# Inputs and output laid out by numpy, a row per partition for each transfer, in a memory attention and mixer kernel

## The chip, the cores and the metric

The kernel runs on 1 core of one Trainium2 chip. The metric is the device time of one execution in microseconds (us); the host's work before and after it, numpy's included, is not in it.

## The reference, cut to what matters

```
a    = softmax(phi, over the sequence)              # phi (8, 8, 576, 32)
k_m  = einsum('bhsm,bhsd->bhmd', a, k)              # q, k, v (8, 8, 576, 64)
v_m  = einsum('bhsm,bhsd->bhmd', a, v)
attn = softmax(q @ k_m.T / 8, over the 32 memories)
x    = (attn @ v_m) as (8, 576, 512)                # heads side by side
h    = relu(x.T @ w_tok1) @ w_tok2                  # 576 -> 256 -> 576
u    = x + h.T
out  = u + relu(u @ w_ch1) @ w_ch2                  # 512 -> 1536 -> 512
```

There are 8 batches of 8 heads. The inputs q and k are scaled up by 64 and phi by 3.18; the four weights arrive as float64.

## The kernel before

**Numbers.** Each large matmul is made of three, with a high and a low part of each operand (`uh`/`ul`, `c1h`/`c1l`, `hh`/`hl` and so on). ACT rounds the high part, DVE or POOL subtracts it for the low part. A float64 weight is read as pairs of 32-bit words, and five passes over 1024 pairs put one fp32 number together (class `Piece`): `low_bits` (ACT, L667), `join` (DVE, L673), `signs` (ACT, L679), `magnitude` (DVE L685 or ACT L683) and `apply` (DVE, L690). Then `part_high` (ACT, L697) and `part_low` (POOL or DVE, L701) split it.

**Heads.** The four heads of one batch with the same parity Q are a `Quad`. It goes through: maximum of phi over the sequence (`_red`, L310; turned on PE and reduced, `phi_turn` L983, `phi_diag` L987 and L989, `phi_spread` L993), subtraction (`phi_sub`, L324), exp; the memories `kvp` from k, v and phi (`mm_kv`, L1002); their scaling, `T` and `vb` (L369 to L409); the keys, turned on PE (`Tp`, L1012) and copied to `kb` (L1016); the scores `sp` from q and `kb` (L1047); softmax on DVE (`S`, L466 to L496); and the token mixer (`nat`, `A`, `R`, `u`), which writes u as `uh` and `ul` (L624, L630).

**Rows.** The 4608 rows of u go through the channel mixer in 9 chunks of 512 (`Chunk`). `ch1` makes one of 12 products `cp` in 12 matmuls of 128x512 (L157), ACT and DVE take its relu as `hh` and `hl`, and `ch2` adds it into four sums `acc` (12 matmuls, L190). At a chunk's end `add` (L208) makes the output `o`, channels on partitions. `turn` (L214) transposes it into `rows` on DVE, and `store` (L224) sends it with 4 DMAs.

**The order.** Every load is issued by SP, in one queue. In the first part (batches 0 and 1, the weights, chunk 0) each operation is a `step` with an engine, a cost in us, steps that it comes after, buffers that it takes (`Room`), and for a load a `move`, the time that its bytes are thought to need. `plan(SEED)` sorts them: it runs a clock over the engines, takes the ready step of highest rank, and adds a random share to the ranks, drawn from `SEED`. `SHARES` says how often a step goes to its other engine. Where the plan has a gap on PE, matmuls of `ident` with itself fill it (L949). What comes after chunk 0 follows a table by hand, `at(h, fn)`, at half-steps h of the products; `run` works it off.

**Transfers.** q of the first two batches lands with the sequence on partitions; `q_turn` transposes it on PE (L1024 into `qp`, the last 64 rows at L1029 into `qt`), and `q_get` copies it to `qT` on ACT (L1036, L1037). Later batches load q in 16 DMAs of 36 KB, and DVE transposes it. The 576 rows of k, v and phi are 4.5 times 128, and so each is loaded as a body and a tail, k apart from v. w_ch1 comes in four DMAs of 32 partitions a piece. The last chunk is done in two halves: four times matmuls, `add` and `turn`, then four DMAs, two from SP's queue and two from ACT's.

Of the kernel before, what the change touches and what calls it, by code (L numbers as in the profile page):

```python
# [20 lines left out]
P = 128  # L21
# [7 lines left out]
def kernel(  # L29
# [3 lines left out]
    k: bass.AP,  # L33
    v: bass.AP,
    phi: bass.AP,
    w_tok1: bass.AP,
    w_tok2: bass.AP,
# [15 lines left out]

    nc = tc.nc

    B, H, S, D = q.shape
    M = phi.shape[3]
    DM = H * D
    TT = w_tok1.shape[1]
    FF = w_ch1.shape[1]  # L60
# [3 lines left out]
    NF = FF // P  # L64
    NT = TT // P
    FULL = S // P
    TAIL = S - FULL * P
    NC = FULL + 1
# [3 lines left out]
    rows_out = out.rearrange("b s e -> (b s) e")  # L72
# [63 lines left out]
    class Chunk:  # L136
# [73 lines left out]
        def turn(s, a, w=slice(0, CW)):  # L210

            if a == 0 and not w.start:
                s.rows = wide(F32, "rows" + s.n).rearrange("p a n -> p (a n)")
            nc.vector.transpose(  # L214
                out=s.rows.rearrange("p (b a t) -> p b a t", a=NKK, t=32)[
                    :, w.start // 32 : w.stop // 32, a, :
                ],
                in_=s.o[:, a, w].rearrange("p (b t) -> p b t", t=32),
            )

        def store(s, w=slice(0, CW), engines=(nc.sync,)):
            rows = s.rows.rearrange("p (b e) -> p b e", e=P)
            for eq in range(4):
                engines[eq % len(engines)].dma_start(  # L224
                    out=rows_out[
                        s.c * CW + w.start : s.c * CW + w.stop, eq * P : (eq + 1) * P
                    ].rearrange("(b t) e -> t b e", t=32),
                    in_=rows[32 * eq : 32 * eq + 32, w.start // 32 : w.stop // 32],
                )
# [16 lines left out]
    class Quad:  # L246
# [3 lines left out]
        def load_phi(s):  # L250
            s.pt = sb.tile([P, 4, NC, M], F32, tag="phi", name="phi" + s.n, bufs=2)
            src = phi[s.b].rearrange("(i z) s m -> z i s m", z=2)[s.Q]
            nc.gpsimd.memset(s.pt[TAIL:, :, FULL, :], FLOOR)
            nc.sync.dma_start(
                out=s.pt[:, :, :FULL, :].rearrange("p i j m -> p i (j m)"),
                in_=src[:, : FULL * P].rearrange("i (p j) m -> p i (j m)", j=FULL),
            )
            nc.sync.dma_start(
                out=s.pt[:TAIL, :, FULL, :],
                in_=src[:, FULL * P :].rearrange("i p m -> p i m"),  # L260
            )

        def load_kv(s):
# [4 lines left out]
            for x in range(0, 4, m):  # L268
# [5 lines left out]
                for z, src in enumerate((k, v)):  # L274
                    src = src[s.b].rearrange("(i z) s d -> z i s d", z=2)[s.Q, x : x + m]
                    nc.sync.dma_start(
                        out=t[:, :, z, :FULL, :].rearrange("p i j d -> p i (j d)"),
                        in_=src[:, : FULL * P].rearrange("i (p j) d -> p i (j d)", j=FULL),
                    )
                    nc.sync.dma_start(  # L280
                        out=t[:TAIL, :, z, FULL, :],
                        in_=src[:, FULL * P :].rearrange("i p d -> p i d"),
                    )
                s.kv += [t[:, i] for i in range(m)]

        def load_q(s):

            s.qr = sb.tile([P, 4, HALF], F32, tag="qT", name="q" + s.n, bufs=1)
            src = q[s.b].rearrange("(i z) s d -> z i s d", z=2)[s.Q]
            for g in range(4):  # L290
                hf, db = g // 2, g % 2
                for i in range(4):
                    nc.sync.dma_start(
                        out=s.qr[32 * g : 32 * g + 32, i].rearrange("p (a d) -> p a d", d=32),
                        in_=src[
                            i, hf * HALF : (hf + 1) * HALF, db * 32 : db * 32 + 32
                        ].rearrange("(a t) d -> t a d", t=32),
                    )

        def q_turn(s):  # L300
            s.qT = sb.tile([P, 4, HALF], F32, tag="big", name="qT" + s.n, bufs=1)
            for i in range(0, 4, 2):
                nc.vector.transpose(
                    out=s.qT[:, i : i + 2].rearrange("p i n -> p (i n)"),
                    in_=s.qr[:, i : i + 2].rearrange("p i n -> p (i n)"),
                )
# [328 lines left out]
    def place(ap):  # L635
        return ap.bitcast(I32)

    class Piece:
# [12 lines left out]
        def load(s, room):  # L651
# [8 lines left out]
            for part in s.parts:  # L660
                part.raw = at[:, n : n + part.words]
                part.load(part.raw)
                n += part.words
            s.low, s.high = at[:, :n, 0], at[:, :n, 1]
# [40 lines left out]
    class PartW1:  # L705


        loads = 2

        def __init__(s, c):  # L710
            s.c, s.n, s.name = c, (1 if c else FULL), f"w1_{c}"
            s.words, s.move = s.n * TT, (1.1 if c else 4.3)

        def load(s, raw):
            c, n = s.c, s.n
            if c:
                for x in range(0, P, TAIL):
                    nc.sync.dma_start(
# [20 lines left out]
    class PartW2:  # L739
        words, loads, move = NT * HALF, 2, 2.7  # L740

        def __init__(s, hf):
            s.w, s.name = slice(hf * HALF, (hf + 1) * HALF), f"w2_{hf}"
# [772 lines left out]
```

## Time and profile before

| | us |
|---|---|
| median of 3 runs | 803.11 (803.10 to 803.45) |
| span of the profiled execution | 798.4 |
| that execution's own time | not listed |
| PE busy | 774.9 (97%) |
| DVE busy | 407.5 (51%) |
| ACT busy | 227.3 (28%) |
| POOL busy | 133.2 (17%) |
| bytes moved | 66.40 MB, in 172472 packets |

The span runs from the first to the last event of the device's records; the rest of the run's time lies outside it. An engine's busy time is the union of its instructions, without waiting. In the rows of the trace that follow, a row is: start or line, duration or engine, the operation, output<-input, partitions x elements and type, xcount, and in brackets or behind the last bar the idle time before it with what ended it. PEld is the loading of weights into PE, SPq and ACTq are the DMA queues of those engines.

### The profile page before, as it was taken

Reading aid. Unit: us, or ns where it says so; the run is one execution under the profiler, and the core shown is the slowest. Engines: PE = TensorE matmul, PEld = TensorE weight load, DVE = VectorE, ACT = ScalarE, POOL = GpSimd, SP = SyncE. Lnnn points to the kernel's source line nnn. Section 1 sums busy time; section 2 is a strip of 40 time slices with the busy share of each in tenths; the row PEclk is TensorE's granted clock in tenths of the full one; section 3 lists DMA queues with packets and bytes.
Section 4 is the critical chain, followed back from the end, with each engine's and each line's share of the span. In section 5 each row is a group of like instructions: output and inputs, shape, how many; then the busy total and the mean of one; then the engine's idle time right before and its main releaser. Section 6 shows DMA issues by size and latency. Waiting matters only on the chain.

```text
span 798.4 us, 11998 instructions
## 1 busy us (share of the span) xinstructions
PE 774.9 (97%) x4727; PEld 643.2 (81%) x4727; DVE 407.5 (51%) x704; ACT 227.3 (28%) x421; POOL 133.2 (17%) x129
## 2 busy tenths in 40 slices
PE   6799999999999999999999999999999999999997
PEld 5587778888887878788878888888878888888886
DVE  4899964576538453645455535645373413212115
ACT  4596654332222222121213122222222211111010
POOL 2145222311131003100301012101300300202000
PEclk9899999999999999999999999999999999999999
DMA  8999273226514433171505260535124101100202
GB/s 220 240 249 261 63 182 82 60 60 128 117 22 108 85 80 60 40 153 21 119 10 130 55 135 3 122 71 117 23 42 77 30 1 25 30 0 1 53 0 53
DMA packets 172472, 66.40 MB, mean 83 GB/s; under 512 B 115456, under 2 KB 166656, under 8 KB 172416
## 3 DMA queue, kind: packets, MB, share of 16 engines
q1 hardware_dynamic: 171328, 65.11, 36.4%
q8 instruction: 37, 0.61, 0.3%
q10 hardware_dynamic: 1088, 0.52, 0.3%
q14 instruction: 19, 0.16, 0.1%
HBM read 52.30 MB, written 13.30 MB: 82 GB/s over the span
## 4 chain that ended last, share of the span: by engine, by line
PE 81%; DVE 7%; DMA 4%; SPq 3%; issue 3%; POOL 1%; ACT 1%; POOLq 0%; DVEq 0%; ACTq 0%
PE cp L157 33%; PE acc L190 32%; PE u L609 8%; PE Ap L569 3%; DMA rawc<-in_moe_w_ch_dram 3%; PE Rp L588 1%; DVE o L208 1%; PE end L190 1%; PE kvp L357 1%; DMA phi<-in_phi_dram 1%; SPq L970 1%; DVE hl L127 1%; PE sp L458 1%; SPq L280 1%; DVE S L490 1%
## 5 line engine op out<-in xcount | busy, mean ns | idle before, releaser
L190 PE MATMUL acc<-hh,c 128*128 128x512 f32 x832 | 278.2, 394 | 0.7
L127 DVE SCALAR_TENSOR_TENSOR hl<-cp,hh 128x512 fp32r<-128x512 f32 x104 | 71.6, 689 | 246.3 <-ACT hh L124 246.1
L190 PEld LDWEIGHTS acc<-hh,c 128*128 128x128 f32 x832 | 156.2, 188 | 39.1 <-issue 4.9
L157 PE MATMUL cp<-uh,c1h 128*128 128x512 f32 x432 | 163.6, 392 | 0.0
L157 PE MATMUL cp<-ul,c1h 128*128 128x512 f32 x432 | 162.5, 390 | 0.0
L157 PE MATMUL cp<-uh,c1l 128*128 128x512 f32 x432 | 162.3, 389 | 0.0
L190 PE MATMUL acc<-hl,c 128*128 128x512 f32 x416 | 162.3, 390 | 0.0
L124 ACT ACTIVATE hh<-cp 128x512 fp32r<-128x512 f32 x104 | 62.0, 597 | 293.5 <-PE cp L157 290.2
L157 PEld LDWEIGHTS cp<-uh,c1l 128*128 128x128 f32 x432 | 81.1, 188 | 17.0
L157 PEld LDWEIGHTS cp<-ul,c1h 128*128 128x128 f32 x432 | 81.2, 188 | 16.6
L157 PEld LDWEIGHTS cp<-uh,c1h 128*128 128x128 f32 x432 | 80.4, 188 | 17.0 <-issue 0.9
L190 PEld LDWEIGHTS acc<-hl,c 128*128 128x128 f32 x416 | 78.3, 188 | 13.8
L202 POOL TENSOR_TENSOR o<-uh,ul 128x512 f32<-128x512 f32 x36 | 48.1, 1362 | 117.0 <-DMA out_dram<-rows 46.7
L504 POOL TENSOR_TENSOR al<-aT,ah 128x576 fp32r<-128x576 f32 x16 | 25.4, 1588 | 237.3 <-ACT ah L500 212.8
L310 DVE TENSOR_REDUCE pr<-phi 128x128 f32<-128x640 f32 x27 | 35.6, 1317 | 20.9 <-DMA phi<-in_phi_dram 12.8
L609 PE MATMUL u<-w2l,Rh 128*128 128x288 f32 x128 | 37.8, 295 | 0.0
L609 PE MATMUL u<-w2h,Rl 128*128 128x288 f32 x128 | 37.7, 295 | 0.0
L609 PE MATMUL u<-w2h,Rh 128*128 128x288 f32 x128 | 37.8, 295 | 0.0
L569 PE MATMUL Ap<-w1h,nat 128*128 128x256 f32 x144 | 28.0, 286 | 3.1 <-DVE nat L1072 2.4
L127 DVE SCALAR_TENSOR_TENSOR Rl<-Rp,Rh 128x512 fp32r<-128x512 f32 x16 | 11.0, 690 | 35.6 <-ACT Rh L124 35.6
L630 DVE TENSOR_TENSOR ul<-u,uh 128x288 fp32r<-128x288 f32 (+8 forms) x48 | 16.7, 355 | 22.4 <-ACT uh L624 22.3
L343 POOL PARTITION_ALL_REDUCE psr<-pr x11 | 12.2, 1107 | 92.6 <-issue 46.4
(153 smaller groups left out, 944.6 us busy)
## 6 DMA issues: line engine op xcount, KB each, us to landing
out_dram<-rows SPq DMA_DIRECT2D x32, 256.0 KB, 4.5
kv<-in_k_dram SPq DMA_DIRECT2D x15, 512.0 KB, 5.5
kv<-in_v_dram SPq DMA_DIRECT2D x15, 512.0 KB, 6.8
q<-in_q_dram SPq DMA_DIRECT2D x192, 36.0 KB, 2.2
rawc<-in_moe_w_ch_dram SPq DMA_DIRECT2D x24, 256.0 KB, 8.6
rawc<-in_moe_w_ch_dram SPq DMA_DIRECT2D x12, 512.0 KB, 5.8
phi<-in_phi_dram SPq DMA_DIRECT2D x16, 256.0 KB, 3.7
rows<-S SPq DMA_DIRECT2D x48, 72.0 KB, 2.0
```

The lines of the kernel that those rows point to most:

```text
L124: nc.scalar.activation(out=h, in_=ps, func=AF.Relu)
L127: nc.vector.scalar_tensor_tensor(out=l, in0=ps, scalar=0.0, in1=f32(h), op0=ALU.max, op1=ALU.subtract)
L157: nc.tensor.matmul(ps, l[:, a, w], r[:, a], start=n == 0, stop=n == len(mm) - 1)
L190: nc.tensor.matmul(ps, l_[f // 2][:, f % 2, a * P : (a + 1) * P], r[:, w], start=f == start and x == 0, stop=f == end - 1 and x == 2,)
L202: nc.gpsimd.tensor_tensor(out=s.o[:, a], in0=f32(s.uh[:, a]), in1=f32(s.ul[:, a]), op=ALU.add)
L208: nc.vector.tensor_tensor(out=o, in0=ps or s.acc[a], in1=o, op=ALU.add)
L310: nc.vector.tensor_reduce(out=m.rearrange("p (i m) -> p i m", i=4), in_=s.pt.rearrange("p i j m -> p i m j"), axis=AX.X, op=op,)
L343: nc.gpsimd.partition_all_reduce(s.r, m, P, RED.add)
L504: eng.tensor_tensor(out=s.al, in0=s.aT, in1=f32(s.ah), op=ALU.subtract)
L569: nc.tensor.matmul(ps[:, :TT], a, w, start=x == 0, stop=x == len(mm) - 1)
L609: nc.tensor.matmul(ps[:, :HALF], a, r, start=x == 0, stop=x == len(mm) - 1)
L630: nc.vector.tensor_tensor(out=ch.ul[:, kk, to], in0=ps[:, :n], in1=f32(ch.uh[:, kk, to]), op=ALU.subtract)
```

## The change

Numpy (`_lay`) lays every input out so that one transfer is one row of contiguous bytes for each of the 128 partitions:

- q comes turned, channels on partitions. `q_turn` and `q_get` are gone, on PE, ACT and DVE.
- k and v are one array, padded with zeros to 640 rows, phi is padded with `FLOOR`. A quad's phi is one DMA, its k and v one.
- The weights come as 64-bit words, a piece's words together. The channels are in another order: w_ch1's rows and w_ch2's columns are permuted by `_channels`.
- The output is stored by channels, straight from `o`; `turn` is gone. Numpy turns it back. In the last chunk each group of channels is stored behind its own `add`, from SP and ACT in turn.
- The planner's costs for SP and its `move`s are new, `part_high` of a piece's second part comes after that of its first, and `SEED` goes from 423 to 334. The first part is so planned anew.

```diff
+def _channels(np):
+    return np.arange(512).reshape(4, 4, 32).transpose(1, 0, 2).reshape(4, P)
...
-        def turn(s, a, w=slice(0, CW)):
...
-        def store(s, w=slice(0, CW), engines=(nc.sync,)):
...
+        def store(s, w=slice(0, CW), channels=slice(0, NKK), eng=nc.sync):
+            eng.dma_start(out=out[s.c, :, channels, w], in_=s.o[:, channels, w])
...
         def load_phi(s):
             s.pt = sb.tile([P, 4, NC, M], F32, tag="phi", name="phi" + s.n, bufs=2)
...
+            nc.sync.dma_start(out=s.pt, in_=phi[s.b, s.Q])
...
+                nc.sync.dma_start(out=t, in_=kv[s.b, s.Q, :, x : x + m])
...
+            nc.sync.dma_start(out=s.qT.rearrange("p i n -> p (i n)"), in_=q[s.b, s.Q])
...
     class PartC1:
-        words, loads, move = 2 * DM, 4, 4.4
+        words, loads, move = 2 * DM, 1, 2.75
...
-            for x in range(4):
-                nc.sync.dma_start(
-                    out=raw[32 * x : 32 * x + 32].rearrange("p (a n) t -> p a (n t)", a=NKK),
-                    in_=place(w_ch1[x * P : (x + 1) * P, s.w]).rearrange("(a c) n -> c a n", c=32),
-                )
+            nc.sync.dma_start(out=raw.rearrange("p (a n) t -> p a (n t)", a=NKK), in_=w_ch1[s.f // 2])
...
-    NOISE, SEED = 0.3, 423
+    NOISE, SEED = 0.3, 334
...
-            s.l_phi = step("SP", 1.25, s.load_phi, take=[s.phi], move=1.2)
-            s.l_kv = step("SP", 2.5 * len(s.kvs), s.load_kv, take=s.kvs, move=3.5 + len(s.kvs))
-            s.l_q = step("SP", 3.1, s.load_q, take=[s.qroom], move=2.6)
+            s.l_phi = step("SP", 0.62, s.load_phi, take=[s.phi], move=0.9)
+            s.l_kv = step("SP", 0.62 * len(s.kvs), s.load_kv, take=s.kvs, move=3.5)
+            s.l_q = step("SP", 0.62, s.load_q, take=[s.qroom], move=1.6)
...
-            s.x_q0 = z = step("PE", 1.0, lambda: s.q_turn(0, [b0, b1]), s.l_q, take=[b0, b1], use=[s.qroom])
-            z0 = step("ACT", 0.9, lambda: s.q_get(0), z, take=[qT], use=[b0, b1])
-            s.x_q1 = z = step("PE", 0.7, lambda: s.q_turn(1, [b2]), z0, take=[b2], use=[s.qroom])
-            z1 = step("ACT", 0.62, lambda: s.q_get(1), z, use=[qT, b2])
...
-        for x in range(NKK):
-            at(h + 3 + x // 2 * 2, lambda c=c, x=x: chunks[c].turn(x), k=1)
-        at(h + 6, lambda c=c: chunks[c].store(), k=1)
+        at(h + 3, lambda c=c: chunks[c].store(), k=1)
...
-            last.turn(a, w)
-        last.store(w, (nc.sync, nc.scalar))
+            last.store(w, slice(a, a + 1), (nc.sync, nc.scalar)[a % 2])
```

What the new plan does shows in the order of the engines' rows (line, operation, output<-input, size, count; a name ends in a number of its own). First SP, from the start of the program to the second quad's q: `phi_0` and `phi_1`, `kv_0` and q are those of the two quads of batch 0, `raww` is w_tok1. Before:

```order
L254 DMA phi_0_104<-in_phi_dram 128x4x128
L258 DMA phi_0_104<-in_phi_dram 64x4x32
L724 DMA raww_0_112<-in_moe_w_tok_dram 128x2x512 x2
L276 DMA kv_0_115<-in_k_dram 128x4x256
L280 DMA kv_0_115<-in_k_dram 64x4x64
L276 DMA kv_0_115<-in_v_dram 128x4x256
L280 DMA kv_0_115<-in_v_dram 64x4x64
L970 DMA q_0_131<-in_q_dram 128x4x64 x4
L974 DMA q_0_131<-in_q_dram 64x4x64
```

And after:

```order
L236 DMA phi_0_104<-in_phi_dram 128x640
L236 DMA phi_1_106<-in_phi_dram 128x640
L663 DMA raww_0_108<-in_w_tok_dram 128x2048
L249 DMA kv_0_110<-in_kv_dram 128x2560
L892 DMA q_0_112<-in_q_dram 128x1152
L661 DMA raww_4_114<-in_w_tok_tail_dram 64x512 x2
L249 DMA kv_0_1_119<-in_kv_dram 128x1280
L249 DMA kv_0_1_121<-in_kv_dram 128x1280
L892 DMA q_1_132<-in_q_dram 128x1152
```

The sequence of what is loaded is kept; each thing is one transfer of 128 partitions in place of two to five, and SP has 132 rows in the program for 203. The third piece of w_ch1, `rawc_2_294`, is asked for after 12.3 MB (it stands behind the first q of batch 1) and moves 1.05 MB.

Then PE at the second quad of batch 1, in the middle of chunk 0's products. Before:

```order
L1012 MATMUL Tp_1_1187<-ident,T_1_1179 128x128
L1024 MATMUL qp_1_1_1195<-ident,q_1_468 128x128 x4
L1029 MATMUL qt_1_1200<-ident,q_1_468 128x64 x2
L157 MATMUL cp_0_1204<-uh_590,c1h 128x512 x4
L157 MATMUL cp_0_1204<-ul_591,c1h 128x512 x4
L157 MATMUL cp_0_1204<-uh_590,c1l 128x512 x4
L1024 MATMUL qp_1_1_1223<-ident,q_1_468 128x128 x4
```

And after:

```order
L928 MATMUL Tp_1_1068<-ident,T_1_1056 128x128
L159 MATMUL cp_0_1072<-uh_556,c1h 128x512 x4
L159 MATMUL cp_0_1072<-ul_557,c1h 128x512 x4
L159 MATMUL cp_0_1072<-uh_556,c1l 128x512 x4
L940 MATMUL sp_1_1_1087<-q_1_842,kb_1_1085 64x288 x2
```

The two groups of transposes are gone from both sides of the product, and the scores follow right behind it.

Last DVE, up to the last `ul` of chunk 0's part of u, which is DVE's row 72 before and row 77 after. Before, from row 66:

```order
L630 TENSOR_TENSOR ul_591<-u_0_0_609,uh_590 128x224
L690 SCALAR_TENSOR_TENSOR rawc_2_338<-rawc_2_338 128x1024
L630 TENSOR_TENSOR ul_591<-u_0_1_626,uh_590 128x288
L310 TENSOR_REDUCE pr_0_667<-phi_0_415 128x128
L630 TENSOR_TENSOR ul_591<-u_0_1_654,uh_590 128x288
L630 TENSOR_TENSOR ul_591<-u_0_1_640,uh_590 128x224
L630 TENSOR_TENSOR ul_591<-u_0_1_669,uh_590 128x224
```

And after, from row 61 to 72 (`rawc` are pieces of w_ch1 and w_ch2):

```order
L619 SCALAR_TENSOR_TENSOR rawc_2_294<-rawc_2_294 128x1024
L636 SCALAR_TENSOR_TENSOR rawc_0_151<-rawc_0_151 128x1024
L636 SCALAR_TENSOR_TENSOR rawc_0_156<-rawc_0_156 128x1024
L129 SCALAR_TENSOR_TENSOR Rl_1_534<-Rp_1_509,Rh_1_529 128x512
L903 TENSOR_REDUCE mc_0_536<-mt_0_531 128x1
L905 TENSOR_SCALAR dg_0_538<-ident,mc_0_536 128x128
L619 SCALAR_TENSOR_TENSOR rawc_4_160<-rawc_4_160 128x1024
L579 TENSOR_TENSOR ul_557<-u_0_0_469,uh_556 128x288
L579 TENSOR_TENSOR ul_557<-u_0_0_518,uh_556 128x224
L579 TENSOR_TENSOR ul_557<-u_0_1_540,uh_556 128x288
L579 TENSOR_TENSOR ul_557<-u_0_0_483,uh_556 128x224
L259 TENSOR_REDUCE pr_1_593<-phi_1_300 128x128
```

Behind these stand four more `ul` and, among them, the subtraction of phi (L273). So all of phi's rows for the third quad, one more reduction of phi and one more pass over a piece's words (a magnitude) stand ahead of the last `ul`, and fewer rows of the weights behind it; the number of DVE's rows in the first part is the same.

More of the change, by code (lines that the diff above doesn't have):

```diff
@@ L54 @@
     nc = tc.nc
[L56 to L60, printed above, removed]
+    w_tok1, w_tok1_tail, w_tok2, w_ch1, w_ch2 = (
+        w.bitcast(I32) for w in (w_tok1, w_tok1_tail, w_tok2, w_ch1, w_ch2)
+    )
+    B, _, _, _, _, NC, D = kv.shape
+    M = phi.shape[5]
+    FULL, TAIL = NC - 1, w_tok1_tail.shape[0]
+    S = FULL * P + TAIL
+    DM = w_ch2.shape[3] // 2
+    TT = w_tok1.shape[2] // 2
+    NF = 2 * w_ch2.shape[0]
+    FF = NF * P
     HALF = S // 2
@@ L632, in u_low @@
                 )
-    def place(ap):
-        return ap.bitcast(I32)
     class Piece:
@@ L785 @@
     class PartC2:
-        words, loads, move = DM, 1, 2.2
+        words, loads, move = DM, 0.5, 1.375
         held = []
@@ L1254, in piece @@
             us = 0.12 + 1.08e-3 * part.words
-            h = step("ACT", us, lambda x=x: p.part_high(x), z, take=part.rooms(), use=[raw])
+            h = step(
+                "ACT", us, lambda x=x: p.part_high(x), z, *(y[0] for y in out),
+                take=part.rooms(), use=[raw],
+            )
             l = step(
```

210 lines of the change are left out of this document (69 added, 141 removed).

## The prediction

> **What bounds the kernel now.** I read the whole page first, then busy time by stage, then what TensorE (PE) and VectorE (DVE) wait for in the first two stages, then the loads, then the last microseconds. The page's first line:
>
> ```profile
> span 798.4 us, 11998 instructions
> ```
>
> The median of the runs is 803.11, so 4.7 us lie outside the span of the profiled execution (803.1 - 798.4); its own time isn't listed, and I take 798.4 + 4.7 = 803.1 as its time. Busy time by stage (stretch, its length, busy time of PE, PEld, DVE, ACT, POOL, then granted PE clock, DMA share, GB/s):
>
> ```profile
> 0.00:4.50 4.50, 2.50 (x10) 2.21 (x10) 0.00 (x0) 1.49 (x2) 1.92 (x21) 1.00 0.45 109
> 4.50:21.10 16.60, 11.16 (x122) 8.42 (x123) 10.53 (x19) 8.36 (x13) 2.41 (x1) 0.92 1.00 248
> 21.10:56.30 35.20, 28.64 (x258) 23.95 (x257) 31.34 (x55) 27.17 (x48) 12.03 (x9) 0.94 1.05 253
> 56.30:100.00 43.70, 41.69 (x268) 32.54 (x267) 41.20 (x49) 30.74 (x43) 17.27 (x11) 1.00 0.66 162
> 100.00:149.20 49.20, 48.19 (x336) 40.82 (x335) 26.58 (x47) 24.53 (x43) 14.39 (x9) 1.00 0.43 107
> 234.20:319.00 84.80, 84.66 (x513) 70.36 (x512) 44.06 (x85) 19.49 (x41) 11.52 (x12) 1.00 0.37 78
> 792.70:798.40 5.70, 0.00 (x0) 0.00 (x0) 0.86 (x2) 0.00 (x0) 0.00 (x0) 0.84 0.44 93
> ```
>
> Four regimes stand in these rows. Up to 56.3 (stage one: batch 0 and the weights) PE is not the limit: DVE works 31.34 of the last 35.20, with the DMA queues full (share 1.00 and 1.05). From 56.3 to 149.2 (stage two: chunk 0's products beside batch 1's heads) PE is busy 89.88 of 92.90, yet DVE is at 41.20 of 43.70 in its first half. In the later loop (a batch in 84.80) PE is idle for 0.14. At the end 5.7 us pass in which PE does nothing.
>
> The first product of chunk 0 needs all of u, and so waits for the last `ul`, its low part:
>
> ```profile
> 55.22 1.05 DVE L630 TENSOR_TENSOR ul<-u,uh 128x288 fp32r<-128x288 f32 x3
> ```
>
> The last of these three ends at 55.22 + 1.05 = 56.27. PE begins chunk 0 just there, so stage one is as long as DVE's row of instructions up to that `ul`.
>
> **A: stage one, +3.6.** DVE becomes dense with the first transpose of scores, at 21.15; before it the chain runs from k and v over `kvp` to the scores `sp`, on PE:
>
> ```profile
> 13.66 0.43 PE L1002 MATMUL kvp<-kv,phi 128*32 128x128 f32 x8 [1.17 <-issue]
> ```
> ```profile
> 18.75 3.08 PE L1047 MATMUL sp<-qT,kb 128*64 128x288 f32 x8 [0.82 <-ACT kb L1016]
> ```
> ```profile
> 113.05 1.19 PE L1047 MATMUL sp<-qT,kb 128*64 128x288 f32 x8
> ```
> ```profile
> 21.15 0.47 DVE L466 STREAM_TRANSPOSE S<-sp 128x288 f32<-128x288 f32 x1
> ```
>
> And how fast the loads come (stretch, length, clock, DMA share, GB/s):
>
> ```profile
> 6.50:9.00 2.50, 1.00 1.00 366
> 30.00:38.00 8.00, 0.87 1.08 219
> 41.00:43.50 2.50, 1.00 1.03 408
> ```
>
> The three stretches carry w_tok1 (rows of 2048 bytes in a partition), w_ch1 (a quarter of the partitions at a time) and w_ch2 (rows of 4096). The queues are full in all; what differs is the form of the transfer. Every load of after is one piece over 128 partitions, of 2.3 KB a partition or more, so I take 387, the middle of 366 and 408 (bounds 219 and 408). Up to `kv_0` SP asks for 3.02 MB: 0.49 are moved by 4.5 (4.5 x 109), the other 2.53 take 6.5 at 387, so k and v are there at 11.0 (at 11.4 by 366) where `kvp` begins at 13.66 now; with 0.2 for its start, 2.4 earlier. The q transposes on PE and their copies on ACT go: 0.75 of the 0.82 that `sp` waits for `kb`, which stands behind a copy of `qT`. And `sp` took 3.08 here and 1.19 later; being earlier and without the stop before it, it may get the fuller clock: 1.2 of the 1.89, an estimate. Together 4.4.
>
> Against it stands what the new order puts ahead of the last `ul` on DVE: 77 rows for 72. No instruction is added in stage one; five are moved up:
>
> ```profile
> L690 DVE SCALAR_TENSOR_TENSOR rawc<-rawc 128x1024 f32<-128x1024 f32 x12 | 16.0, 1334 | 1.1 <-ACT rawc L679 1.0
> L673 DVE SCALAR_TENSOR_TENSOR rawc<-rawc 128x1024 int32<-128x1024 int32 x12 | 15.5, 1295 | 1.5 <-ACT rawc L667 1.4
> L127 DVE SCALAR_TENSOR_TENSOR hl<-cp,hh 128x512 fp32r<-128x512 f32 x12 | 8.2, 685 | 4.2 <-ACT hh L124 4.1
> L685 DVE TENSOR_SCALAR rawc<-rawc 128x1024 int32<-128x1024 int32 x7 | 7.3, 1037 | 0.1
> L310 DVE TENSOR_REDUCE pr<-phi 128x128 f32<-128x640 f32 x5 | 6.5, 1291 | 6.7 <-DMA phi<-in_phi_dram 6.7
> L324 DVE TENSOR_TENSOR phi<-phi,mb 128x640 f32<-128x640 f32 x5 | 4.0, 814 | 0.2 <-PE mb L993 0.2
> ...
> L989 DVE TENSOR_SCALAR dg<-ident,mc 128x128 f32<-128x128 f32 x5 | 1.4, 287 | 0.2
> L987 DVE TENSOR_REDUCE mc<-mt 128x1 f32<-128x128 f32 x5 | 1.4, 285 | 1.3 <-PE mt L983 1.2
> ```
>
> One of each of the last five: 1.04 + 1.29 + 0.81 + 0.29 + 0.29 = 3.7 later. Then the gaps: between 21.1 and 56.3 DVE stands for 35.20 - 31.34 = 3.86. The new order puts other rows between the steps that wait for each other (the scales of the second quad between two steps of the first one's softmax, for one), and no load is asked for late; I take 2.9 of it away and leave 1.0. So A = 4.4 - 3.7 + 2.9 = **3.6**. Bounds: with the loads' 2.4 alone and no gap filled 2.4 - 3.7 = -1.3; with all of both 4.4 - 3.7 + 3.9 = 4.6. I take the value near the upper end, since waits of DVE in the new rows have other rows ahead of them to hide in.
>
> **B: q's transposes in stage two, +2.8; C: waits there, +2.2.** Grouped by form from 56.3 to 149.2 (count, busy time, mean ns, idle before), and what PE waited for there (sum, times, longest):
>
> ```profile
> L1047 PE MATMUL sp<-qT,kb 128*64 128x288 f32 x16 | 3.1, 422 | 0.2 <-ACT qT L1037 0.2
> ...
> L1024 PE MATMUL qp<-ident,q 128*128 128x128 f32 x16 | 2.5, 276 | 0.4 <-ACT kb L1016 0.4
> ...
> L1029 PE MATMUL qt<-ident,q 64*128 64x64 f32 x4 | 0.6, 241 | 0.4 <-issue 0.4
> ```
> ```profile
> 75.64 0.60 PE L1024 MATMUL qp<-ident,q 128*128 128x128 f32 x4
> 76.00 0.48 PE L190 MATMUL acc<-hh,c 128*128 128x512 f32 x1
> ```
> ```profile
> PE Ap L569 <- DVE nat L1072: 1.4, 1, 1.4
> PE Tp L1012 <- DVE vb L392: 0.7, 1, 0.7
> PE qt L1029 <- issue: 0.4, 1, 0.4
> PE qp L1024 <- ACT kb L1016: 0.4, 1, 0.4
> PE sp L1047 <- ACT qT L1037: 0.2, 1, 0.2
> ```
>
> The 20 transposes of batch 1's q are busy for 2.5 + 0.6 = 3.1, of which about 0.7 overlaps the matmul behind each of the four groups (0.24 in the row shown: begun at 75.64, 0.60 long, the next at 76.00); the 0.4 of issue inside them goes too: 3.1 - 0.7 + 0.4 = **2.8**. Nothing takes their place, since q lands turned. Bounds: 2.4 without the issue, 3.5 without the overlap, and 0 if DVE holds the stage (a rival).
>
> The other waits are 1.4 + 0.7 + 0.4 + 0.2 = 2.7. To these comes what the `sp` of quad (1, 0) is stretched: 16 of them take 3.1 where 8 take 1.19, so 3.1 - 2.4 - 0.2 is up to 0.6 more that the list doesn't name. What hangs on `qT`'s copies goes for certain, 0.8 to 0.9. The others hang on DVE's and ACT's chains, which lose rows ahead of them; I take half of their 2.5. C = 0.9 + 1.3 = **2.2**, bounds 0 and 3.4. What is late next is PE itself: it does 89.88 - 2.8 of work in the stage.
>
> **D: the later loop, 0.** DVE loses the transposes of the output (four a chunk) and of q (two a quad), SP many of its issues, but PE is idle for only 0.14 in 84.80 and hides all of it. Without that cover DVE would be the measure, and it works 44.06 of 84.80. k, v and phi grow by their padding, a ninth, where the queues' share is 0.37. Bounds 0 and 0.14 a batch, six times.
>
> **E: the end, +1.5.**
>
> ```profile
> 793.15 0.45 DVE L214 STREAM_TRANSPOSE rows<-o 128x256 f32<-128x256 f32 x1
> 793.62 0.81 SPq L224 DMA_DIRECT2D out_dram<-rows  x2
> ```
>
> Now the last half waits until all of its four transposes are done, and then four transfers leave, two to a queue. After the change each group of channels leaves behind its own addition. The last transpose goes (0.45), the second issue on the queue too (half of 0.81, 0.4), and one transfer of 128 KB is in flight at the end in place of four; of the 798.43 - 793.62 = 4.8 that they take, I count 0.65 as queueing. Sum **1.5**, bounds 0.4 (the transpose alone) and 2.2 (1.3 of queueing).
>
> **Sum.** 3.6 + 2.8 + 2.2 + 0 + 1.5 = 10.1; 803.1 - 10.1 = **793.0**. The last `ul` then ends at 56.27 - 3.6 = 52.7.
>
> **Rivals.**
> Loads that stay slower, the rival on the other side. DVE's 61st row in the new order (the join of the third piece of w_ch1) stands 17 rows ahead of the last `ul`. From it on these rows take 5.3 (four passes like L690 and L673) + 0.7 (`Rl`, as long as `hl`) + 2.8 (eight `ul` at 1.05 / 3) + 2.7 (phi's rows above) = 11.5; with 0.8 for gaps and longer `ul` it is due at 52.7 - 12.3 = 40.4. Ahead of it goes a pass of ACT over the loaded words:
>
> ```profile
> 55.42 1.26 ACT L667 ACTIVATE rawc<-rawc,mask 128x1024 f32<-128x1024 uint32 x1
> ```
>
> Up to that piece SP asks for 13.37 MB, 12.88 after 4.5. At 387 they land at 37.8, and the pass ends at 39.1: in time. At 366 it is 0.6 late, at 330, between there and the break-even, 4.4: 797.4. From about 288 GB/s down all of the 10.1 is lost (12.88 MB in 44.7, landing at 49.2), and below it the kernel is **slower** than before; at 253, the mean of stage one now, the pass ends at 56.7, 16.3 late: 809. For it: stage one's mean is 253. Against it: that mean comes from stretches like 30 to 38 (219), whose form goes, and 366 and 408 stand where the form is the new one.
> The Trainium skill ("DMA: Bandwidth & Descriptors", section "Bandwidth") gives 341 GB/s for a transfer of 1 MB and about 358 as one core's share of the memory; by 341 the piece would be 3.2 late, an estimate of 796.2. The rows of 366 and 408 are above both figures, so the trace weighs against it as a ceiling.
>
> DVE holds stage two: it is busy 41.20 of 43.70 in the first half, and if PE merely waits elsewhere for it, B and C are hidden: 803.1 - 5.1 = 798.0. For it: that row, and the wait for `nat`. Against it: the 3.7 that DVE does ahead of the last `ul` it no longer does behind it, so it has 37.5 left there.
>
> The clock. Stage one's is 0.92 and 0.94 on average, and `sp` at 3.08 for 1.19 shows what a slow stretch costs: 1.89 a quad. Fewer filling matmuls stand ahead of `kvp` (4 for 9); if both quads fall into slow stretches and my 1.2 isn't got, A loses 2 to 4: 795 to 797. The Trainium skill ("TensorE: Matmul & The Clock Gate", Part 1) has the clock rise after some 3.4 us of steady work, and fall again after an idle stretch as long, in windows that run freely; by it, fewer fills speak for the lower clock. The trace shows such halves, but can't show where they fall in the new order.
>
> Better than forecast: A, B, C and E at their best bounds give 1.0 + 0.7 + 1.2 + 0.7 = 3.6 more, 789.4; less than that only if `kvp` waits on something that I don't see and that goes too.
>
> **Chances.** The forecast, 789.5 to 795.5: 0.59. Loads between 288 and 366, 795.5 to 801: 0.10. Loads below, slower: 0.06. DVE in stage two, 796 to 800: 0.12. The clock, 795 to 797: 0.08. Under 789.5: 0.05. The range 789.5 to 798.5 holds the first, the clock, and most of the loads and DVE cases: 0.82. A measurement of this kernel can tell 0.2% (1.6 us) from no change: faster than 801.5 is 0.90, within 0.04, slower than 804.7 0.06.
>
> **What would show it.** The last `ul` ends near 52.7 and `kvp` begins near 11.3; the load rate from 5 to 40 is above 360; DVE stands about 1 us between the first transpose of scores and the last `ul`. From there to chunk 1's first product it is 88 (92.9 now), and the list of PE's waits there is about 1.5 long, without `qt` and `qp`. A batch takes 84.8 as before. From the last addition to the end it is 3.8, not 5.3. I am wrong if a pass of ACT over weights waits for its DMA past 40, if DVE's rows leave gaps where PE's chain of u is late, or if `nat` and `vb` keep PE waiting as long as now.

## The result, and the profile after

| | before | after |
|---|---|---|
| time, median (range), us | 803.12 (803.10 to 803.45, 4 runs) | 790.30 (788.12 to 792.62, 4 runs) |
| span of the profiled execution | 798.43 | 790.44 |
| that execution's own time | not listed | 792.35 |
| PE / DVE busy | 774.9 / 407.5 | 769.9 / 367.0 |

The ratio is 0.985, with a 95% interval from 0.9825 to 0.9876: faster, by 1.2 to 1.8%. The four times after are two pairs, 792.35 and 792.62, and 788.25 and 788.12; the profile is of the first.

Busy time by stage of the kernel after, in the columns of the same view of before (PE, PEld, DVE, ACT, POOL, granted clock, DMA share, GB/s), cut at the events that answer to those there:

```profile
0.00:4.50 4.50, 2.50 (x10) 2.21 (x10) 0.68 (x1) 1.49 (x2) 1.58 (x19) 1.00 0.57 182
4.50:19.80 15.30, 10.05 (x107) 8.20 (x109) 9.08 (x18) 6.08 (x9) 1.89 (x1) 1.00 1.00 355
19.80:54.90 35.10, 27.35 (x262) 24.10 (x260) 32.90 (x60) 27.31 (x47) 12.34 (x8) 1.00 0.67 274
54.90:100.00 45.10, 45.10 (x359) 36.83 (x359) 38.19 (x54) 32.08 (x43) 17.35 (x10) 1.00 0.43 160
100.00:143.50 43.50, 42.17 (x229) 35.13 (x228) 23.80 (x37) 22.05 (x36) 13.20 (x9) 1.00 0.23 83
230.30:315.10 84.80, 84.64 (x513) 70.35 (x512) 40.10 (x75) 19.50 (x41) 11.49 (x10) 1.00 0.27 82
787.40:790.40 3.00, 0.00 (x0) 0.00 (x0) 0.07 (x1) 0.00 (x0) 0.00 (x0) 1.00 0.22 73
```

Between the first transpose of scores and the last `ul` DVE now works 32.90 of 35.10 (31.34 of 35.20 before), in stage two PE works 87.27 of 88.60, a batch of the later loop takes what it took, and the end is 3.0 long. The marks, in the timelines of PE and DVE after, are the memories, the scores, the first transpose of scores, the last `ul` and the first product of chunk 1:

```profile
13.40 0.65 PE L918 MATMUL kvp<-kv,phi 128*32 128x128 f32 x8 [3.39 <-DMA kv<-in_kv_dram]
```
```profile
18.56 2.19 PE L940 MATMUL sp<-q,kb 128*64 128x288 f32 x8 [0.35 <-ACT kb L932]
```
```profile
19.83 0.48 DVE L415 STREAM_TRANSPOSE S<-sp 128x288 f32<-128x288 f32 x1 [1.63 <-PE sp L940]
```
```profile
54.55 0.37 DVE L579 TENSOR_TENSOR ul<-u,uh 128x224 fp32r<-128x224 f32 x1
```
```profile
143.50 0.39 PE L159 MATMUL cp<-uh,c1h 128*128 128x512 f32 x1
```

`kvp_0` (the memories of the first quad) waits 3.39 for k and v and begins only 0.26 earlier than before; the scores take 2.19, between the two values of before, 3.08 and 1.19. The last `ul` ends at 54.92.

PE ran at half pace in the first part of stage one. The clock column reads 1.00 there, since the trace has no record of the clock before its first change at 22.7; the pace is read from like rows of `kvp`, of the first quad and of the second:

```profile
15.64 0.65 PE L918 MATMUL kvp<-kv,phi 64*32 64x128 f32 x8
22.86 0.42 PE L918 MATMUL kvp<-kv,phi 64*32 64x128 f32 x8
```

The prediction has chunk 0 wait for the last `ul`; it does not. PE around its first product, before and after:

```profile
55.36 0.33 PE L983 MATMUL mt<-ident,pr 128*128 128x128 f32 x1 [0.46 <-DVE pr L310]
55.45 1.18 PE L157 MATMUL cp<-uh,c1h 128*128 128x512 f32 x4
56.47 1.08 PE L157 MATMUL cp<-ul,c1h 128*128 128x512 f32 x4
```
```profile
54.68 0.71 PE L873 MATMUL mt<-ident 128*128 128x128 f32 x4 [1.42 <-DVE phi L273]
55.26 1.17 PE L159 MATMUL cp<-uh,c1h 128*128 128x512 f32 x4
56.27 1.07 PE L159 MATMUL cp<-ul,c1h 128*128 128x512 f32 x4
```

The first four matmuls read `uh` alone. Those that read `ul` follow without a gap, and the last `ul` is ready when they begin (it ends at 56.27 before and at 54.92 after). What stands ahead of the product in PE's queue is `mt`, the turn of a quad's maxima of phi (before the third quad's, after the fourth's), and that is what waits for DVE: before for the reduction `pr`, after for the subtraction of the third quad's phi at L273, with four filling matmuls behind the wait. So PE's chunk 0 begins at 55.45 before and at 55.26 after, only 0.19 earlier.

What PE waited for behind it, in stage two, and the rate of the loads from 17 to 40:

```profile
PE mb L909 <- DVE dg L905: 0.7, 1, 0.7
PE np L953 <- DVE phi L273: 0.5, 1, 0.5
```
```profile
17.00:40.00 23.00, 1.00 1.02 416
```

All five waits of before are gone from stage two, and two short ones have come. The end, in the timeline after (`o` is the last sum):

```profile
787.04 0.42 DVE L210 TENSOR_TENSOR o<-end,o 128x256 f32<-128x256 f32 x1 [0.65 <-PE end L192]
787.50 0.34 ACTq L213 DMA_DIRECT2D out_dram<-o  x1
```

One transfer is issued right behind the last addition. From its end at 787.46 (before: 793.12) to the end of the span it is 2.98 (5.31).

From span to span the steps come to (in the first row up to the end of the last `ul`, as the prediction counts):

| stretch | before | after | gain |
|---|---|---|---|
| start to the last `ul` | 56.27 | 54.92 | 1.35 |
| last `ul` to chunk 1's first product | 92.92 | 88.58 | 4.34 |
| from there to PE's end | 643.46 | 643.50 | -0.04 |
| PE's end to the end | 5.78 | 3.44 | 2.34 |
| sum | 798.43 | 790.44 | 7.99 |

Cut at chunk 0's first product in place of the last `ul`, the first two gains are 0.19 and 5.50. The medians differ by 12.8. Where the other 4.8 are is the first question of the experiments.

### The profile page after: what moved, and what is told of

Read it like the earlier page. It is cut to its first block, busy times and chain, and to the rows that moved or that the text cites. A ratio compares the mean times of both kernels' runs of the same rounds, so it can differ in the third digit from the quotient of the medians.

```text
span 790.4 us, 11371 instructions
## 1 busy us (share of the span) xinstructions
PE 769.9 (97%) x4699; PEld 641.6 (81%) x4699; DVE 367.0 (46%) x640; ACT 223.9 (28%) x410; POOL 125.7 (16%) x112
## 3 DMA queue, kind: packets, MB, share of 16 engines
HBM read 54.92 MB, written 13.30 MB: 86 GB/s over the span
## 4 chain that ended last, share of the span: by engine, by line
PE 85%; DVE 10%; DMA 3%; issue 1%; ACT 1%; SPq 0%; DVEq 0%; ACTq 0%
PE cp L159 35%; PE acc L192 33%; PE u L558 8%; PE Ap L518 3%; DMA kv<-in_kv_dram 1%; PE kvp L918 1%; PE Rp L537 1%; DVE o L210 1%; DMA rawc<-in_w_ch_dram 1%; PE end L192 1%; PE kvp L306 1%; DVE rawc L619 1%; DVE S L439 1%; DVE S L415 1%; DVE sm L434 1%
## 5 line engine op out<-in xcount | busy, mean ns | idle before, releaser
L453 POOL TENSOR_TENSOR al<-aT,ah 128x576 fp32r<-128x576 f32 x15 | 22.0, 1467 | 226.5 <-ACT ah L449 223.2
L292 POOL PARTITION_ALL_REDUCE psr<-pr x11 | 12.2, 1107 | 94.4 <-DVE pr L259 41.3
L449 ACT CAST ah<-aT 128x576 fp32r<-128x576 f32 x16 | 10.8, 676 | 57.6 <-DVE aT L445 57.6
## 6 DMA issues: line engine op xcount, KB each, us to landing
rawc<-in_w_ch_dram SPq DMA_DIRECT2D x12, 1024.0 KB, 10.1
```

The lines of the kernel that those rows point to most:

```text
L292: nc.gpsimd.partition_all_reduce(s.r, m, P, RED.add)
L449: nc.scalar.copy(out=s.ah, in_=s.aT)
L453: eng.tensor_tensor(out=s.al, in0=s.aT, in1=f32(s.ah), op=ALU.subtract)
```

## The experiments

**The kernel before once more**, to see its own time beside its span.

> The kernel before, unchanged, to see its own time beside its span. The changed kernel's profiled execution took 792.35 with a span of 790.4, so 1.95 lie outside the span. Theory 1 (what lies outside the span shrank with the change): span 798.4, time 803.1, 4.7 outside. Theory 2 (the listed profile of before was of a faster execution than its timed runs): span about 801.2, 1.95 outside.

Nine runs lay between 800.14 and 805.24 (median 801.33), and the profiled one had 805.24 with a span of 803.47: 1.77 outside the span, as after (792.35 - 790.44 = 1.91). Theory 2 holds, though not with the span that it names. So the profile that the prediction was read from was that of an execution of about 798.43 + 1.8 = 800.2, 2.9 faster than the median beside it. The rest of the 4.8 is that the profile after is one of the slower pair (792.35, the median 790.30). This trace also shows what made this one execution 5.0 slower than the profile of before. DVE's timeline, and PE's windows (busy time, clock, DMA share, GB/s):

```profile
56.74 1.32 DVE L310 TENSOR_REDUCE pr<-phi 128x128 f32<-128x640 f32 x1 [1.70 <-DMA phi<-in_phi_dram]
```
```profile
59.40:62.80 3.40, 3.40 (x9) 0.50 0.71 161
```

The phi of the third quad lands late, and its reduction stands ahead of three `ul` in DVE's queue: the last `ul` ends at 59.03, 2.8 later than in the other profile. Then comes a stretch of 3.4 at half clock in the products themselves. Whether the other slow runs of this kernel have the same causes is not known.

**More filling matmuls, and none**, in stage one of the kernel after:

```diff
+    a.x_p1.fill, c.x_p1.fill, a.x_kv.fill = 7, 1, 16
     for z in order:
         now[0] = z
```

> The changed kernel with more filling matmuls ahead of the first quad's memories: 7 for 5 ahead of the first mt, 1 ahead of the second, 16 for 4 ahead of kvp_0, so that PE works nearly without a stop from 1.6 to 13.4. Theory (the runs at 792.4 and at 788.2 differ by the time at which PE comes up to full clock: at 22.5 or before the first scores): every run at 788 or a little less, the eight matmuls of a kvp group 0.28 apart and not 0.53, the first product of chunk 0 at about 51. Rival (the two differ in how fast the loads land): the runs split as before, 788.2 and 792.4, whatever the fill.

```diff
     for z in order:
+        if z.eng == "PE" and z.begin < a.x_s[1].begin:
+            z.fill = 0
         now[0] = z
```

> The changed kernel without any filling matmul up to the second scores of the first quad. Theory (late clock): 792 to 794 in every run, never 788, kvp and sp of the first quad at half speed. Rival (loads): the same split of 788.2 and 792.4.

With more of them 791.61 (791.03 to 791.76); without any 792.15 and 792.31; the kernel before, measured beside them, stood at 801.80. `kvp_0`'s groups did get the full clock with more (0.28 to 0.30 apart against 0.53), but the first scores came at 18.54, as in the kernel after, and the first product at 54.52, not 51. The gain was lost in two places. The fills themselves held `kvp_0` back: k and v, asked for at 2.09, landed 8.0 later, at 10.1, while PE was busy with fills until 13.19. The row of the loads (its last number is the time from issue to landing), and PE:

```profile
kv<-in_kv_dram SPq DMA_DIRECT2D x1, 1280.0 KB, 8.0
```
```profile
8.68 4.51 PE L873 MATMUL kvp<-ident 128*128 128x128 f32 x29
13.11 0.43 PE L918 MATMUL kvp<-kv,phi 128*32 128x128 f32 x8
```

And right behind `kvp_0` DVE lost time, in the timelines of DVE and POOL:

```profile
15.39 1.76 DVE L320 TENSOR_SCALAR ms<-mask,ps 128x6 f32<-128x6 f32 x1
```
```profile
14.74 2.40 POOL L647 TENSOR_TENSOR w1l<-raww,w1h 128x1024 fp32r<-128x1024 f32 x1 [12.12 <-ACT w1h L643]
```

DVE's 0.23 of work takes 1.76, to 17.15, and POOL's subtraction ends at 17.14. And from 17.81 to 21.22 the granted clock was half, so that the scores took 2.19 again. The expected 788 did not come, nor did the split into pairs: neither theory holds as it was put. Without fills the 792 and the half pace came that the theory names, but the kernel after runs at half pace there too, so that trial decides nothing.

**The end as before**: transposes, then four transfers a half.

```diff
-            last.store(w, slice(a, a + 1), (nc.sync, nc.scalar)[a % 2])
+            nc.vector.transpose(out=rows..., in_=last.o[:, a, w]...)
+        for eq in range(4):
+            (nc.sync, nc.scalar)[eq % 2].dma_start(
+                out=out[last.c, 32 * eq : 32 * eq + 32, :, w], in_=rows...)
```

> The changed kernel whose last chunk is transposed in blocks of 32 on DVE again and leaves by four transfers of 32 partitions behind the half's last transpose (its output of that chunk is not turned back). Theory (the end's gain of 2.3 is the transposes and the batched transfers): 2.3 slower in the span, 2.97 from the last addition to the end becoming about 5.3. If what lies outside the span hangs on the last transfers too, 5.0 slower in time; if on the number of descriptors of the whole program, 2.3 slower in time with 2.0 outside the span.

From the last addition to the end it is 5.56 (2.98 after, 5.31 before), 2.58 more; 1.79 lie outside the span. So the end's gain is the transposes and the batched transfers together, and nothing of it lies outside the span. The median was 793.65.

**The kernel after again**, twice.

> The changed kernel, unchanged, beside the others. Theory 1 (its runs differ by the phase of the clock's windows in stage one): single times spread from 788 to 793 on one chip, the median near 790. Theory 2 (by chip): all of them within 0.5 of each other.

> The changed kernel again, to stand beside the other two on their chip: 789.8 to 792.6 on the chips so far, with one pair at 788.2.

790.74 (789.84 to 791.39) and 790.69 (789.71 to 791.09), with the kernel before at 801.56 and 802.15 beside them: 10.8 and 11.5 faster. Neither theory is met: the times spread over 1.5. `kvp_0` began at 12.26 and 12.47 there, 1.1 and 0.9 earlier than in the first profile, and the last `ul` ended at 53.92 and 53.63, 1.0 and 1.3 earlier. The first product of chunk 0 came at 54.25 and 53.96. The pace of PE was the same in all three, half until 21 to 22.7. What remains between the three profiles is when k and v land: from `kvp_0` to the last `ul` they need 41.5, 41.7 and 41.2. The pair at 788.2 was never met again; no trace of it is at hand, and its cause is open.

**The seed of before, 423**, in the kernel after.

> The changed kernel planned with the seed of before, 423, and nothing else undone: the new costs, layouts and stores stay. Theory 1 (the layout carries the gain; the seed is one draw among good ones): within 1.5 of the changed kernel. Theory 2 (the seed was picked for a plan that is luckier on the chip): 2 to 5 slower, the last ul of chunk 0 ending at 57 or later in place of 54.9.

793.93, 3.2 slower than the kernel after measured beside it (the profile is of its fastest run, 792.50). `kvp_0` began at 10.85, 1.4 earlier, and DVE reached the scores at 16.77, 1.9 earlier; yet the last `ul` ended at 55.40, 1.5 later. DVE's windows up to that `ul`, of the kernel after measured beside it and of this one (length, busy time and count, clock, DMA share, GB/s):

```profile
0.00:53.92 53.92, 42.66 (x78) 1.00 0.75 294
```
```profile
0.00:55.40 55.40, 44.58 (x78) 0.97 0.74 286
```

As many instructions, 1.9 more of work. Where it goes shows in the timelines of DVE and POOL:

```profile
18.71 2.05 DVE L425 TENSOR_TENSOR S<-S,mx 128x576 f32<-128x576 f32 x1
```
```profile
17.73 2.42 POOL L647 TENSOR_TENSOR w1l<-raww,w1h 128x1024 fp32r<-128x1024 f32 x1 [15.13 <-ACT w1h L643]
```

A subtraction of 0.75 takes 2.05 and ends 0.6 behind POOL's, which is what it needs by itself; the same subtraction of the second quad takes 1.05, again beside POOL. The two are 1.6 of the 1.9. So theory 2 holds in the time (3.2, in its 2 to 5), though not in the last `ul` (55.40, not 57): against this one other draw the plan carries 3 of the 11. The rows beside POOL are part of that; from the scores to the last `ul` this plan needs 38.6 where the kernel after needs 35.2, and 3 rows of DVE that the other does earlier stand in that stretch.

**Ten transposes a quad back on PE** in stage two.

```diff
             s.sp.append(ps)
+            if s.b == 1:
+                for x in range(5):
+                    nc.tensor.transpose(ps[:, :P], s.qT[:, 0, :P], ident)
```

> The changed kernel with ten transposes a quad put back on PE in stage two (five ahead of each half of the scores, into the bank that the scores then overwrite; nothing reads them). Theory (B: PE carries stage two, so its work there counts in full): 2.4 to 2.8 slower; from the first product of chunk 0 to that of chunk 1 about 90.8 in place of 88.2. Rival (DVE carries it): under 0.5 slower.

794.08, 3.3 slower. The group of the transposes, and the first product of chunk 1:

```profile
L941 PE MATMUL sp<-ident,q 128*128 128x128 f32 x20 | 2.9, 275 | 0.0
```
```profile
145.23 0.39 PE L159 MATMUL cp<-uh,c1h 128*128 128x512 f32 x1
```

From the first product of chunk 0 (54.52) it is 90.71, and 88.15 to 88.28 in the three profiles of the kernel after: of 2.9 of added work 2.4 to 2.6 count. PE carries stage two, as B has it.

**k, v and q first**, ahead of w_tok1, planned anew with that.

```diff
-    first_loads = [a.l_phi, c.l_phi, loads[0], a.l_kv, a.l_q, loads[1], c.l_kv, c.l_q, *loads[2:5]]
+    first_loads = [a.l_phi, c.l_phi, a.l_kv, a.l_q, loads[0], loads[1], c.l_kv, c.l_q, *loads[2:5]]
```

> The changed kernel with k and v and q of the first quad asked for ahead of w_tok1, and planned anew with that. Theory (A fell short since kvp_0 waits for k and v, which landed at 13.4 among other loads): kvp_0 begins near 10, the first transpose of scores near 16 in place of 19.8, the last ul ends 3 to 4 earlier, 3 to 4 faster. Rival (DVE's row of work in stage one is what is long, and it now stands waiting for w_tok1): within 1 of the changed kernel.

794.45, 3.7 slower. The memories begin at 10.07 as expected, and it does not help. PE, DVE and POOL in the profile of it; its own time was 798.06, the slowest of four, the others 794.3 to 794.6:

```profile
10.07 0.65 PE L918 MATMUL kvp<-kv,phi 128*32 128x128 f32 x7 [1.17 <-DMA kv<-in_kv_dram]
```
```profile
52.63 3.46 DVE L636 SCALAR_TENSOR_TENSOR rawc<-rawc 128x1024 f32<-128x1024 f32 x1
```
```profile
52.57 2.45 POOL L647 TENSOR_TENSOR c1l<-rawc,c1h 128x1024 fp32r<-128x1024 f32 x1 [9.00 <-ACT c1h L643]
```

A pass of 1.2 begins 0.06 behind POOL's and takes 3.46: 2.4 of standing until POOL is done at 55.02, and then 1.07 of its own. The last `ul` ends at 60.87, and DVE's window up to it has 6.0 more of busy time than that of the kernel after, for as many instructions:

```profile
0.00:60.87 60.87, 48.67 (x78) 0.90 0.68 261
```

Neither theory names this: in this execution what DVE meets on the way outweighs an earlier start. The granted clock is lower there too (0.75 from 20 to 30 and 0.83 from 40 to 50; the kernel after has the full clock from 22.7 on), and how much of all this the three faster executions have is not known. The trial changes the order of the loads and the plan at once, so what the loads' order alone is worth stays open.

**w_ch1 in quarters** of the partitions again, over the new layout.

```diff
-            nc.sync.dma_start(out=raw.rearrange("p (a n) t -> p a (n t)", a=NKK), in_=w_ch1[s.f // 2])
+            for x in range(0, P, 32):
+                nc.sync.dma_start(
+                    out=raw[x : x + 32].rearrange("p (a n) t -> p a (n t)", a=NKK),
+                    in_=w_ch1[s.f // 2, x : x + 32],
+                )
```

> The changed kernel with each piece of w_ch1 asked for in four transfers of 32 partitions, as before, over the new layout. Theory 1 (the form is what held the loads at 219 GB/s): from 17 to 40 the rate falls from 416 to below 330, pieces land 2 to 4 later; since DVE's first pass over the third piece stands at 44.5 in its queue and its load is in well ahead, 0 to 1 slower. Theory 2 (short rows in memory held them): the rate stays near 400 and the time the same. The prediction's rival (below 366 the third piece is late one for one): 3 or more slower if the rate falls to 300.

812.57, 21.9 slower than the kernel after measured beside it and slower than the kernel before (ratio 1.0145, 1.0112 to 1.0177). The rates, and what ACT waited for from 17 to 66 (sum, times, longest):

```profile
17.00:40.00 23.00, 0.86 1.02 276
40.00:56.00 16.00, 0.88 0.83 227
```
```profile
ACT rawc L613 <- DMA rawc<-in_w_ch_dram: 16.0, 4, 8.7
```

The form of the transfer sets the rate (416 to 276, both with full queues and rows of 8 KB), and the rate sets the time. This is the prediction's rival on the other side, and it is dearer than priced there (its sum gives 805 for 276): ACT's queue is in order, so its first pass over a piece that isn't there holds back the copies and exponentials of both quads behind it. (Behind the longest wait, of 8.7, the high part of `A` comes only at 53.78.) The last `ul` ends at 65.87, 12.2 later, and stage two is 6.0 longer.

**Filling matmuls, and POOL behind vb.** To take away what the first trial with fills ran into, POOL's subtraction waits for `vb`, which comes behind `ms`:

```diff
+    a.x_p1.fill, c.x_p1.fill, a.x_kv.fill, a.x_T.fill = 7, 1, 16, 8
+    def low_behind_vb(fn=w1[1].fn):
+        gate = sb.tile([P, 8], F32, tag="gate", name="gate", bufs=1)
+        nc.gpsimd.tensor_tensor(out=gate, in0=a.vb[:, :8], in1=a.vb[:, :8], op=ALU.add)
+        fn()
+    w1[1].fn = low_behind_vb
+    order.remove(w1[1])
+    order.insert(1 + next(x for x, z in enumerate(order) if z.fn == a.spread_v), w1[1])
```

> The filling matmuls of the first trial, 8 more in place of 3 ahead of the first turn of T, and the low part of w_tok1 on POOL made to wait for the first quad's vb (a small sum that reads it), so that POOL no longer works beside DVE's ms. Theory (that trial lost what it won to POOL, whose 2.40 ran to 17.15 just as DVE's ms, 1.76 for 0.23, and then to a half-speed stretch from 17.8): ms takes 0.23 again, the scores 1.19 and not 2.19, the first transpose of scores at 17.5 or earlier, the last ul at 52.0 to 52.9, 788 to 789. Rival (DVE's row behind it is the limit, whatever comes ahead): 790 to 791, as the changed kernel.

799.13, 8.4 slower than the kernel after. In stage one what was expected came in part: `ms` takes 0.23, the scores 1.19, the last `ul` ends at 53.20. But from the first product of chunk 1 to PE's end it took 651.35 in place of 643.4. The only thing that is new there is the tile `gate`, of 32 bytes in each partition, behind which `hh`, `hl` and other buffers lie 32 bytes further on (`hh` begins at byte 217056 of a partition in place of 217024). So the sum was written into `w1l`, where the subtraction overwrites it, and the tile left out:

```diff
-        gate = sb.tile([P, 8], F32, tag="gate", name="gate", bufs=1)
-        nc.gpsimd.tensor_tensor(out=gate, in0=a.vb[:, :8], in1=a.vb[:, :8], op=ALU.add)
+        nc.gpsimd.tensor_tensor(out=w1l[:, 0, :8], in0=a.vb[:, :8], in1=a.vb[:, :8], op=ALU.add)
```

> The trial with filling matmuls and the low part of w_tok1 behind vb once more, its small sum now written into w1l (which the low part then overwrites) and not into a tile of its own of 32 bytes a partition. That tile moved the buffers behind it (hh, hl and others) by 32 bytes. Theory 1 (the place of those buffers is what made every matmul of the later loop some 1% longer): a chunk with a batch's heads takes 84.8 again and not 85.7, from the first product of chunk 1 to PE's last 643.4 and not 651.4, and the time is 789 to 790.5. Theory 2 (PE at full clock from 10.6 on, or the wait itself, costs the loop its speed): 797 to 801 as there. Whether a median below the changed kernel's 790.7 is left hangs on stage one, where the last ul ended 0.4 to 1.7 earlier.

790.76 (789.84 to 791.39), and 643.42 for that stretch. The matmuls that read `hh`, and those of `uh` with `c1h`, from 235 to 760, with the tile and without it (count, busy time, mean ns of one, idle before):

```profile
L192 PE MATMUL acc<-hh,c 128*128 128x512 f32 x624 | 211.5, 398 | 0.7
L159 PE MATMUL cp<-uh,c1h 128*128 128x512 f32 x312 | 122.7, 393 | 0.0
```
```profile
L192 PE MATMUL acc<-hh,c 128*128 128x512 f32 x637 | 212.4, 393 | 0.7
L159 PE MATMUL cp<-uh,c1h 128*128 128x512 f32 x316 | 123.1, 389 | 0.0
```

Theory 1 holds: the place of the buffers made the difference. For stage one, the rival of the first of the two holds: with PE at full clock from about 10 on, and DVE at the scores at 18.31 in place of 18.70 and 18.90, the last `ul` ends at 53.48, no better than the 53.63 of the kernel after. It isn't quite a trial of the clock alone: POOL's subtraction, now later, stands beside a subtraction of 0.4 on DVE, which takes 1.05. No version was found that beats the kernel after.

## Why the prediction was right, and where it missed

The direction, the order of size and the range held (790.3 in 789.5 to 798.5); the sum of 10.1 lies between the 8.0 of the two profiles and the 12.8 of the medians, near the 10.8 and 11.5 of the two later comparisons. That it fits so well is in part luck. Against the profiled execution (792.35) the forecast of 793.0 is off by only 0.7 because a base 2.9 too high and a term A 2.25 too large cancel.

- **The base, off by 2.9.** The prediction took 4.7 us as lying outside the span. It is 1.7 to 2.1 in every execution whose own time and span are known. A profile and a median of other runs were put together as if of one execution; a kernel whose runs lie between 800 and 805 can't be treated so.
- **A, forecast 3.6, measured 1.35** by the last `ul` (2.4 and 2.6 in the two later profiles), **and 0.19 by chunk 0's first product** (1.2 and 1.5).
  - The loads. k and v were expected at 11.0 to 11.4, and the first transpose of scores 4.4 earlier; `kvp_0` began at 13.40, and the transpose came 1.3 earlier. The rate was near the assumed 387 (350 from 4.5 to 13.40, then 416). But by 13.40 0.82 MB (4.5 x 182) + 3.12 MB (8.9 x 350) = 3.9 MB had moved, not the 3.0 that the sum counted: 0.9 MB of what stands behind k and v in the queue had moved before PE could begin. And PE ran at half pace until 22.7. (Nor is every load one piece over 128 partitions, as it says: two of w_tok1's have 64. They stand behind k and v.)
  - DVE's row. It erred the other way: from the scores to the last `ul` DVE works 1.6 longer, 32.9 for 31.3, not 3.7. Four of the five rows stand there and cost 2.7, as counted; the fifth, the magnitude, ran at 11.96, while DVE waited ahead of the scores. And passes that were stretched before are shorter (the four joins 1.22 for 1.34 on average). That the new order puts fewer of them beside POOL is the likely reason; no trial shows it by itself. The gaps fell from 3.9 to 2.2, not to 1.0. That a longer row is paid back by fewer gaps was right in kind.
  - The path. "PE begins chunk 0 just there" misreads its own profile: the first product begins at 55.45, before the last `ul` ends, behind `mt`, which waits for DVE. In the kernel after, that wait hangs on phi's subtraction, and four filling matmuls (0.55) come behind it. The prediction counts neither, and no run took them out.
- **B, forecast 2.8**, by the trial that puts the transposes back 2.4 to 2.6. **B and C together, forecast 5.0, measured 4.34** from the last `ul` on, 5.50 from chunk 0's first product on. Of the 5.50 PE's work is 3.8 (90.73 to 86.91) and its waiting 1.7 (3.01 to 1.33). DVE did not hold the stage: it is busy for 38.19 of 45.10, while PE works every moment of that stretch.
- **D, forecast 0, measured -0.04.** PE hid the transposes that left DVE: DVE's work in a batch fell from 44.06 to 40.10.
- **E, forecast 1.5, measured 2.34**, above its bound of 2.2. The term that was too small is what it calls queueing: beyond the transpose and the issue, 0.85 together, 1.5 was saved, not 0.65. The trial with the end as before puts transposes and transfers back together, so it doesn't part the two.
- **The rivals.** That the loads stay slow, and the kernel gets slower than before, is real: w_ch1 in quarters does it at 276 GB/s. It was priced too low, since the sum asked only for DVE's 61st row, and ACT's queue stands still earlier. DVE holding stage two is refuted by the trial with the transposes. The clock rival came true (half pace until 21 to 22.7 in all three profiles of the kernel after), but not with the loss of 2 to 4 that it was priced at: with the full clock from about 10 the kernel is no faster.

On the loads, the Trainium skill ("DMA: Bandwidth & Descriptors", section "Bandwidth") gives some 358 GB/s as one core's share of the memory and says that it binds such loads; its own 425 for a transfer of 16 MB stands above that, and so do the 416 over 23 us here. On DVE and POOL the trace agrees with the Trainium skill: "SBUF — State Buffer", section "SBUF: two separate sides", says that the two share one pair of ports as a lock, held for a whole instruction, while the other stands. The row of 3.46 beside POOL's 2.45 fits that; what the page says of the lock's inside no run here shows.

## What to carry to other kernels

Lay each load out as one run of bytes in each of the 128 partitions; here asking for a piece in four transfers of 32 partitions cost a third of the rate with full queues, and, through passes that waited for it at the head of an in-order queue, 22 us. When a planner moves work between DVE and POOL, count which instructions will run beside each other, not only how many there are: one seed and another differed by 3 us at the same number of rows, and in the profiles two rows of DVE beside POOL cost 1.6. Ask of a product's start which row of its own engine's queue stands ahead of it, not only which operand comes last. And don't set a profile's span against other runs' median before seeing how the runs of that kernel spread.

## What was not expected of the hardware

A tile of 32 bytes a partition, of no use in the loop, made the loop 1.2% longer (651.35 for 643.42): the buffers behind it began at 32 in place of 0 modulo 64 bytes, and the matmuls that read `hh` took 398 ns on average for 393. Those of `uh` with `c1h`, which did not move, took 393 for 389, so it isn't only the reading of the moved buffers. Whether 64 is the measure, and whether their writing is what suffers, was not tried.

A transfer of k and v that was asked for fourth in its queue did not land when its bytes and those ahead, 3.0 MB, had moved, but when 3.3 to 3.9 MB had, and so at 10.1 to 13.3 in kernels that ask for the same loads in the same order up to it (10.1 with more fills, 10.7 with the other seed, 12.1 and 13.3 in two executions of the kernel after).
